# Finishing two blocks of a four-block quad as one pair, and a third seven-product quad in every chunk: attention folded into a squared-ReLU feed-forward layer

## The chip, the cores and the metric

The kernel runs on one core of one Trainium2 chip. The number that counts is the device time of one launch in microseconds (us). Nothing is shared between cores, and the profile is one execution on the same core. The engines are TensorE (PE, with its weight loads shown as PEld), VectorE (DVE), ScalarE (ACT), GpSimd (POOL) and SyncE (SP, which issues most transfers). The granted clock of PE is listed in the profile as PEclk.

## The reference

For each of four batches with N = 6080 rows and C = 256 channels, an attention over channels is made, and its output goes through a feed-forward layer of width 2048:

```python
qn = q / (np.linalg.norm(q, axis=1, keepdims=True) + 1e-06)
kn = k / (np.linalg.norm(k, axis=1, keepdims=True) + 1e-06)
s = kn.transpose(0, 2, 1) @ qn / tau
a = np.exp(s - s.max(-1, keepdims=True))
a /= a.sum(-1, keepdims=True) + 1e-09
x = v @ a                      # 24320 x 256 in all
h = x @ w_in                   # 256 -> 2048
r = np.maximum(h, 0.0)
return (r * r) @ w_out         # 2048 -> 256
```

## The kernel before, in words

The attention matrix (256 x 256 per batch) is folded into `w_in`, so the long part is two matrix products over 24320 tokens, here called the first and the second layer. Every float32 operand is split into a high and a low part; one product of two tiles is three matmuls (high x high, low x high, high x low).

**Chunks and quads.** Tokens come in 24 chunks, six to a batch: five of 2 x 512 tokens and one of 2 x 480. A chunk has eight quads (index j = 0 to 7). A quad is a 2 x 2 grid of blocks of the hidden layer: two sets of 128 hidden units by two halves of the tokens, called 11, 12, 21, 22. The first layer makes the four blocks with seven products instead of eight (Strassen's way, in Winograd's form): the functions `m1`, `m7`, `m6`, `m2`, `m5`, `m4`, `m3`, in this order, each of three matmuls (`product`, L384). They run in PSUM: `B` and `H` in the two `h` banks, `X` in the bank `x` and `Z` in the bank `z`. `X` and `Z` start as copies of `B`, made by ACT (L447 after `m1`, L455 after `m6`), then further products add to them. `X` ends as block 11 (after `m2`), `Z` as block 12 (after `m3`). Blocks 21 and 22 are made by DVE from a bank and the saved product `m7` (L472).

**Finishing a block.** `block` (L387 to 398) takes 11 or 12 by itself: Relu out of PSUM (L394, ACT), Square (L395, ACT), the high part (L396, ACT), the low part (L397, DVE). Blocks 21 and 22 are one pair of 2 x 512 in `blocks` (L414 to 419): max-and-multiply on DVE (L417; on ACT for j = 6 and 7), high part on ACT, low part on DVE.

**Second layer.** A plain quad gives eight pieces of three matmuls each (`layer2`, L550 in `accumulate`): four blocks times two halves of the output, added up over the quads in four PSUM banks `o00`, `o01`, `o10`, `o11`. For some quads, those of `SJ = (0, 2, 4)` cut to the chunk's `KS`, Strassen's seven products are used for the second layer too: three in the quad's place (`layer2s`: M3, M2, M4), and four (M1, M5, M6, M7) that are added up over the chunk's such quads in an `h` bank and run later in the chunk (`run_later`). Their operands are kept in `D` tiles (`combos`) and split later (`split_later`, L436 and L437). I call such a quad an S quad and the others P quads. Before the change `KS` is 0 for chunks 0 and 1, 2 for chunks 2 to 17 (quads 0 and 2 are S) and 3 for the last batch, chunks 18 to 23 (quads 0, 2 and 4 are S).

**What sets the order.** `plan` is written out by hand: a quad's seven products with the previous quad's pieces at fixed places between them. Side work (scores and folding of the next batch, loads, splits) has due times in quads (`at`) and is put in by `run_side`. Then a list scheduler of the framework moves an instruction whose operands are not ready behind others of its engine; each engine runs its own list strictly in order and waits on semaphores. Buffers come from rotating pools; taking a buffer waits for its last reader.

Of the kernel before, what the change touches and what calls it, by code (L numbers as in the profile page):

```python
# [6 lines left out]
F32 = mybir.dt.float32  # L7
# [11 lines left out]
def tile_channel_attention_relu2_ffn(ctx, tc, kq, vT, tau, w_in, w_out, outT):  # L19
# [18 lines left out]
    DB = 3  # L38
    OB = 6
# [10 lines left out]
    ps_z = ctx.enter_context(tc.tile_pool(name="ps_z", bufs=1, space=bass.MemoryType.PSUM))  # L50
# [52 lines left out]
    def decode_w_in(g):  # L103
        tag = "sq" if g else "g1"
        W = work.tile([P, NH, 2, GW], F32, name=tag, tag=tag, bufs=2 if g else 3)
# [31 lines left out]
    def score_load(b, g, tag="kq"):  # L137
        t = work.tile([P, G, C2], F32, name=tag, tag=tag, bufs={"kq": KB, "g2": 2, "D": DB}[tag])
# [238 lines left out]
    KS = [0 if ci < 2 else 3 if ci >= (B - 1) * NCH else 2 for ci in range(len(chunks))]  # L377
# [9 lines left out]
    def block(q, c, ps, eng, hl=None):  # L387

        T = chunks[q[0]][2]
        r = work.tile([P, HMAX], F32, name="r")  # L390
        if hl is None:
            hl = work.tile([P, 2, HMAX], F32R, name="g1", bufs=3)
        with tc.high_priority():
            nc.scalar.activation(out=r[:, :T], in_=ps[:, :T], func=AF.Relu)  # L394
        nc.scalar.activation(out=r[:, :T], in_=r[:, :T], func=AF.Square)  # L395
        eng(out=hl[:, 0, :T], in_=r[:, :T])  # L396
        nc.vector.tensor_sub(out=hl[:, 1, :T], in0=r[:, :T], in1=hl[:, 0, :T])  # L397
        gs[q, c] = hl[:, 0], hl[:, 1]
        return r

    def strassen(q):
        ci, j = q
        return j in SJ[:KS[ci]]

    def blocks(q):
# [5 lines left out]
        hl = work.tile([P, 2, 2, HMAX], F32R, name="g2", tag="g2", bufs=2)  # L411
        h, l = hl[:, 0, :, :T], hl[:, 1, :, :T]
        if q[1] >= NJ - 2 and KS[q[0]]:
            nc.scalar.activation(out=s, in_=s, func=AF.Relu)  # L414
            nc.scalar.activation(out=s, in_=s, func=AF.Square)
        else:
            nc.vector.scalar_tensor_tensor(out=s, in0=s, scalar=0.0, op0=ALU.max, in1=s, op1=ALU.mult)  # L417
        nc.scalar.copy(out=h, in_=s)  # L418
        nc.vector.tensor_sub(out=l, in0=s, in1=h)  # L419
        for i, c in enumerate(("21", "22")):  # L420
            gs[q, c] = hl[:, 0, i], hl[:, 1, i]
# [3 lines left out]
    def combos(q):  # L425
# [7 lines left out]
        nc.vector.tensor_sub(out=t2, in0=state[q]["r11"][:, :T], in1=t1)  # L433

    def split_of(x, T, hl):
        nc.scalar.copy(out=hl[:, 0, :T], in_=x)  # L436
        nc.vector.tensor_sub(out=hl[:, 1, :T], in0=x, in1=hl[:, 0, :T])  # L437
        return hl[:, 0], hl[:, 1]

    def m1(q):  # L440
# [4 lines left out]
        st["X"] = ps_x.tile([P, HMAX], F32, name="x")  # L445
# [3 lines left out]
    def m6(q):  # L449
# [3 lines left out]
        st["Z"] = ps_z.tile([P, HMAX], F32, name="z")  # L453
# [25 lines left out]
    def m5(q):  # L479
# [358 lines left out]
```

## Time and profile before

| | us |
|---|---|
| median of three timed runs | 2158.8 (2157.32 to 2159.95) |
| profiled execution, device time | 2156.35 |
| its span (first to last instruction) | 2154.6 |
| PE busy in the span | 2139.2 |
| DVE busy | 1733.2 |
| ACT busy | 1659.3 |

The profiled execution lies 2.45 us under the median of the timed runs, and 1.75 us of it lie outside the span. A row of a group reads: line, engine, operation, tile written <- tiles read, shape, count, then the busy time and the mean of one in ns, then the idle time of the engine just before and who ended it. Matmuls overlap, so the mean of one matmul (389 ns) is its way through the array; the pace is the distance between starts. In the chain of waits a row is the start in us, how long the chain stayed there, and how many matmuls it passed.

### The profile page before, as it was taken

What the parts mean: (1) busy time and instruction counts of PE and PEld (TensorE: products, weight loads), DVE (VectorE), ACT (ScalarE), POOL (GpSimd) and SP (SyncE); (2) the same over time, 40 slices, a digit from 0 to 9 for tenths busy, and PEclk for the clock granted to TensorE, in tenths of its full rate; (3) what the DMA queues carried; (4) which work ended last, traced back from release to release, by engine and by line L of the source; (5) the groups of instructions that cost most, each with busy time, mean ns of one, the idle gap of its engine ahead of it and who ended that gap; (6) DMA issues with size and microseconds to landing.
All of it is one profiled execution on the core that took longest, in us unless ns stands there. A gap on an engine that the chain in (4) does not pass through costs nothing.

```text
span 2154.6 us, 27464 instructions
## 1 busy us (share of the span) xinstructions
PE 2139.2 (99%) x9758; PEld 1770.2 (82%) x9758; DVE 1733.2 (80%) x2492; ACT 1659.3 (77%) x2784; POOL 37.7 (2%) x69
## 2 busy tenths in 40 slices
PE   9999999999999999999999999999999999999999
PEld 8778888888888888888888888888888888888887
DVE  6898888787787988878779798897877877878876
ACT  6677778787787877877778878787777778778776
POOL 0111000000000000000000000000000000000000
PEclk9999999999999999999999999999999999999999
DMA  9768655355765655546667555554655654555542
GB/s 357 278 229 316 234 199 201 137 206 209 261 241 180 220 196 199 178 155 230 211 217 258 201 199 211 183 188 153 215 213 203 231 199 170 195 189 180 188 171 87
DMA packets 123176, 446.26 MB, mean 207 GB/s; under 512 B 12928, under 2 KB 29824, under 8 KB 123040
## 3 DMA queue, kind: packets, MB, share of 16 engines
q1 hardware_dynamic: 115744, 406.11, 53.3%
q0 software_dynamic: 7296, 38.41, 4.7%
q8 instruction: 77, 1.26, 0.2%
q14 instruction: 59, 0.48, 0.1%
HBM read 381.16 MB, written 63.31 MB: 206 GB/s over the span
## 4 chain that ended last, share of the span: by engine, by line
PE 94%; ACT 3%; DVE 2%; DMA 0%; issue 0%; SPq 0%; ACTq 0%; DVEq 0%
PE o L550 39%; PE h L384 23%; PE z L384 12%; PE h L550 6%; PE x L384 6%; PE h L173 4%; PE h L292 2%; PE x L173 2%; ACT g L418 0%; DVE s L472 0%; ACT r L394 0%; DMA kq<-kq 0%; DVE hl L85 0%; ACT r L395 0%; ACT g L396 0%
## 5 line engine op out<-in xcount | busy, mean ns | idle before, releaser
L550 PE MATMUL o<-g,wo 128*128 128x512 f32 (+1 forms) x3858 | 1003.9, 389 | 3.7 <-ACT g L418 2.4
L550 PEld LDWEIGHTS o<-g,wo 128*128 128x128 f32 x3858 | 719.3, 188 | 162.4 <-DVE g L419 10.8
L384 PE MATMUL h<-vt,wt 128*128 128x512 f32 (+1 forms) x2304 | 625.2, 389 | 1.2 <-ACT x L447 0.4
L384 PEld LDWEIGHTS h<-vt,wt 128*128 128x128 f32 x2304 | 430.8, 188 | 95.3 <-ACT uM L580 4.2
L397 DVE TENSOR_TENSOR g<-r,g 128x512 fp32r<-128x512 f32 (+1 forms) x384 | 260.6, 681 | 117.1 <-ACT g L396 114.7
L384 PE MATMUL z<-vt,wt 128*128 128x512 f32 (+1 forms) x1152 | 326.3, 390 | 0.9 <-DVE s L472 0.5
L419 DVE TENSOR_TENSOR g<-s,g 128x1024 fp32r<-128x1024 f32 (+1 forms) x142 | 172.1, 1212 | 119.4 <-ACT g L418 119.3
L394 ACT ACTIVATE r<-z 128x512 f32<-128x512 f32 (+1 forms) x192 | 113.5, 591 | 188.1 <-PE z L384 187.5
L384 PEld LDWEIGHTS z<-vt,wt 128*128 128x128 f32 x1152 | 209.9, 188 | 43.8 <-DVE s L472 4.5
L395 ACT ACTIVATE r<-r 128x512 f32<-128x512 f32 (+1 forms) x384 | 240.4, 629 | 5.9
L396 ACT CAST g<-r 128x512 fp32r<-128x512 f32 (+1 forms) x368 | 225.6, 616 | 5.2
L418 ACT CAST g<-s 128x1024 fp32r<-128x1024 f32 (+1 forms) x142 | 147.4, 1038 | 39.3 <-DVE s L417 39.1
L384 PE MATMUL x<-vt,wt 128*128 128x512 f32 (+1 forms) x576 | 161.9, 388 | 0.0
L455 ACT COPY z<-h 128x512 f32<-128x512 f32 (+1 forms) x192 | 110.9, 578 | 36.8 <-PE h L384 35.7
L384 PEld LDWEIGHTS x<-vt,wt 128*128 128x128 f32 x576 | 108.1, 188 | 21.7
L394 ACT ACTIVATE r<-x 128x512 f32<-128x512 f32 (+1 forms) x192 | 113.9, 593 | 14.5 <-DVE D L433 9.3
L153 DVE TENSOR_TENSOR acc<-acc,sq 128x1024 f32<-128x1024 f32 x92 | 112.2, 1220 | 15.6 <-ACT sq L152 13.5
L371 DVE TENSOR_TENSOR vt<-v,vt 128x512 fp32r<-128x512 f32 (+1 forms) x144 | 95.4, 681 | 35.8 <-ACT vt L370 35.7
L417 DVE SCALAR_TENSOR_TENSOR s<-s 128x1024 f32<-128x1024 f32 (+1 forms) x98 | 118.3, 1207 | 0.2
L447 ACT COPY x<-h 128x512 f32<-128x512 f32 (+1 forms) x192 | 111.5, 580 | 3.7 <-PE h L384 3.1
L467 ACT COPY m<-h 128x512 f32<-128x512 f32 (+1 forms) x192 | 111.6, 581 | 1.7 <-PE h L384 0.6
L472 DVE TENSOR_TENSOR s<-z,m 128x512 f32<-128x512 f32 (+1 forms) x142 | 96.6, 680 | 14.7 <-PE z L384 11.6
(154 smaller groups left out, 2406.5 us busy)
## 6 DMA issues: line engine op xcount, KB each, us to landing
wt<-wsc SPq DMA_DIRECT2D x184, 896.0 KB, 4.7
wo<-wop SPq DMA_DIRECT2D x134, 512.0 KB, 5.3
kq<-kq SPq DMA_DIRECT2D x87, 512.0 KB, 5.2
wsc<-wt POOLq DMA_DIRECT2D x32, 896.0 KB, 5.5
v<-vT SPq DMA_DIRECT2D x40, 512.0 KB, 5.2
outT<-uM SPq DMA_DIRECT2D x80, 256.0 KB, 3.3
wo<-wos SPq DMA_DIRECT2D x50, 384.0 KB, 3.5
wo<-wodM SPq DMA_DIRECT2D x64, 256.0 KB, 4.4
```

The costliest lines, as they stand in the source:

```text
L153: nc.vector.tensor_add(out=accs[b], in0=accs[b], in1=sq)
L173: nc.tensor.matmul(out=s[:, h * C:(h + 1) * C], lhsT=l, rhs=r, start=first and h == 0 and n == 0, stop=last and n == len(terms) - 1, skip_ ...
L384: nc.tensor.matmul(out=out[:, :T], lhsT=w[:, l, i], rhs=v[:, r, :T], start=start and n == 0, stop=n == 2, skip_group_check=True)
L394: nc.scalar.activation(out=r[:, :T], in_=ps[:, :T], func=AF.Relu)
L395: nc.scalar.activation(out=r[:, :T], in_=r[:, :T], func=AF.Square)
L396: eng(out=hl[:, 0, :T], in_=r[:, :T])
L397: nc.vector.tensor_sub(out=hl[:, 1, :T], in0=r[:, :T], in1=hl[:, 0, :T])
L417: nc.vector.scalar_tensor_tensor(out=s, in0=s, scalar=0.0, op0=ALU.max, in1=s, op1=ALU.mult)
L418: nc.scalar.copy(out=h, in_=s)
L419: nc.vector.tensor_sub(out=l, in0=s, in1=h)
L467: nc.scalar.copy(out=state[q]["m7"][:, :T], in_=H[:, :T])
L550: nc.tensor.matmul(out=o[:, :T], lhsT=l, rhs=r[:, :T], start=start and k == 0, stop=stop and k == 2)
```

## The change

Four things change together.

1. `X` and `Z` become the two halves of one two-bank tile `x`. Block 11 is no longer finished after `m2`. After `m3`, the last product, one Relu of 2 x 512 takes both out of PSUM, one Square follows, and `pair` makes high and low parts for both (L396, L397, L403, L404 of the changed kernel). The next quad's first copy into `X` now waits for that Relu. The buffers for it: `g2` has three instead of two, `s` two instead of one, a new `t4` takes the extra operand of an S quad, and `g1` and `r` are gone.
2. The products of a quad stand in the order m1, m7, m6, m5, m4, m2, m3.
3. The pieces of the second layer are a queue (`waiting`): after a P quad four pieces stay behind for the quad after the next, after an S quad two. The part that is run is spread over three places, three eighths after `m7`, a quarter after `m6`, the rest after `m4`. `load_wo` is issued 0.4 quads later, the four later products of a chunk are due at 5.7, 6.4, 7.1 and 7.8 quads.
4. `KS` is 3 for every chunk from the third on, so chunks 2 to 17 have three S quads instead of two. The third operand of a later product goes into a `kq` buffer.

The core of the diff:

```diff
-    ps_z = ctx.enter_context(tc.tile_pool(name="ps_z", bufs=1, space=bass.MemoryType.PSUM))
...
-    KS = [0 if ci < 2 else 3 if ci >= (B - 1) * NCH else 2 for ci in range(len(chunks))]
+    KS = [0 if ci < 2 else 3 for ci in range(len(chunks))]
...
+    def squares(x, out, eng):
+
+        if eng is nc.vector:
+            nc.vector.scalar_tensor_tensor(out=out, in0=x, scalar=0.0, op0=ALU.max, in1=x, op1=ALU.mult)
+        else:
+            nc.scalar.activation(out=out, in_=x, func=AF.Relu)
+            nc.scalar.activation(out=out, in_=out, func=AF.Square)
+
+    def pair(q, x, cs):
+        T = chunks[q[0]][2]
+        hl = work.tile([P, 2, 2, HMAX], F32R, name="g2", tag="g2", bufs=GB)
+        h, l = hl[:, 0, :, :T], hl[:, 1, :, :T]
+        nc.scalar.copy(out=h, in_=x)
+        nc.vector.tensor_sub(out=l, in0=x, in1=h)
+        for i, c in enumerate(cs):
+            gs[q, c] = hl[:, 0, i], hl[:, 1, i]
...
     def m1(q):
...
-        st["X"] = ps_x.tile([P, HMAX], F32, name="x")
+        st["XZ"] = ps_x.tile([P, 2, HMAX], F32, name="x")
+        st["X"], st["Z"] = (st["XZ"][:, i] for i in range(2))
...
     def m2(q):
         product(q, A12, state[q]["X"], False)
-        state[q]["r11"] = block(q, "11", state[q]["X"], nc.scalar.copy if KS[q[0]] else nc.vector.tensor_copy)
...
     def m3(q):
         product(q, S4, state[q]["Z"], False)
         T = chunks[q[0]][2]
+        r = work.tile([P, 2, HMAX], F32, name="s", tag="s", bufs=2)
+        with tc.high_priority():
+            squares(state[q]["XZ"][:, :, :T], r[:, :, :T], nc.scalar)
+        pair(q, r[:, :, :T], ("11", "12"))
         if strassen(q):
...
+            t2, t1 = kept[q][:, 0, :T], kept[q][:, 1, :T]
+            nc.vector.tensor_sub(out=t2, in0=r[:, 0, :T], in1=t1)
+            nc.vector.tensor_sub(out=r[:, 1, :T], in0=r[:, 1, :T], in1=t2)
+            hl = work.tile([P, 2, HMAX], F32R, name="t4", tag="t4", bufs=1)
+            gs[q, "t4"] = split_of(r[:, 1, :T], T, hl[:, 0], hl[:, 1])
...
-        for m, t in zip(MS, {0: (), 2: (3.9, 4.7, 5 + MID, 6.2), 3: (5 + MID, 6.2, 6.8, 7 + MID)}[KS[ci]]):
+        for m, t in zip(MS, {0: (), 3: (5.7, 6.4, 7.1, 7.8)}[KS[ci]]):
...
-            at(n - 0.2, load_wo, ci, j)
+            at(n + 0.2, load_wo, ci, j)
...
-    plan = (m1, m7, ("11", 0), ("11", 1), m6, m2, ("21", 0), ("21", 1), m5, m4, ("22", 0), ("22", 1), ("12", 0),
-            m3, ("12", 1))
...
+    plan = (m1, m7, 0, m6, 1, m5, m4, 2, m2, m3)
+    waiting = []
     for n in range(len(quads) + 1):
         q = quads[n] if n < len(quads) else None
         p = quads[n - 1] if n else None
...
+        if p:
+            waiting += ([(layer2s, p, m) for m in ("M3", "M2", "M4")] if strassen(p) else
+                        [(layer2, p, c, e) for c in ("21", "22", "11", "12") for e in range(NH)])
+        todo = max(0, len(waiting) - (2 if p and strassen(p) else 4)) if q else len(waiting)
+        parts = [todo * 3 // 8, todo // 4]
+        parts.append(todo - sum(parts))
```

How it stands on the engines, at the step from quad 2 (S) to quad 3 (P) of chunk 20, in the last batch, where the number of products is the same before and after. PE before: `z_16847` is quad 2's block 12 (its last product `m3`), `h_16898` is `B` of quad 3, `x_16902` and `z_16919` its `X` and `Z`.

```order
L384 MATMUL z_16847<-vt_16616,wt_16719 128x512 x3
L384 MATMUL h_16898<-vt_16320,wt_16793 128x512 x3
L384 MATMUL h_16904<-vt_16362,wt_16793 128x512 x3
L550 MATMUL o10_16803<-g1_16813,wo_16734 128x512 x3
L550 MATMUL o00_16765<-g1_16853,wo_16807 128x512 x3
L384 MATMUL h_16898<-vt_16415,wt_16793 128x512 x3
L384 MATMUL x_16902<-vt_16580,wt_16793 128x512 x3
L550 MATMUL o11_16818<-g1_16813,wo_16734 128x512 x3
L384 MATMUL z_16919<-vt_16589,wt_16793 128x512 x3
```

PE now: the first row is quad 2's `m3` into the second half of its `x` tile; `h_15993` is `B` of quad 3, `x_15997` its two-bank tile, first used by `m5` in its `Z` half.

```order
L384 MATMUL x_15925<-vt_15726,wt_15818 128x512 x3
L384 MATMUL h_15993<-vt_15453,wt_15893 128x512 x3
L384 MATMUL h_15999<-vt_15486,wt_15893 128x512 x3
L545 MATMUL o00_15905<-g2_15918,wo_15873 128x512 x3
L384 MATMUL h_15993<-vt_15531,wt_15893 128x512 x3
L545 MATMUL o01_15966<-g2_15918,wo_15873 128x512 x3
L545 MATMUL o10_15936<-g2_15918,wo_15873 128x512
L384 MATMUL x_15997<-vt_15692,wt_15893 128x512 x3
L384 MATMUL h_15993<-vt_15720,wt_15893 128x512 x3
```

Between `m6` and `m5` there stood six matmuls (`m2` and a piece); now four matmuls of pieces stand there, and between `m3` and the next `m6` there are nine instead of twelve. ACT at the same place before (`r_16890` is block 12 of quad 2, `r_16924` block 11 of quad 3):

```order
L394 ACTIVATE r_16890<-z_16847 128x512
L395 ACTIVATE r_16890<-r_16890 128x512
L447 COPY x_16902<-h_16898 128x512
L467 COPY m7_16908<-h_16904 128x512
L396 CAST g2_16889<-r_16890 128x512
L455 COPY z_16919<-h_16898 128x512
L394 ACTIVATE r_16924<-x_16902 128x512
```

and now (`s_15982` holds blocks 11 and 12 of quad 2):

```order
L396 ACTIVATE s_15982<-x_15925 128x1024
L441 COPY x_15997<-h_15993 128x512
L459 COPY m7_16003<-h_15999 128x512
L397 ACTIVATE s_15982<-s_15982 128x1024
L448 COPY x_15997<-h_15993 128x512
L403 CAST g2_15985<-s_15982 128x1024
```

The copy into `X` (L441) stands directly behind a Relu of twice the width, and the Square of twice the width now stands ahead of the copy into `Z` (L448), which `m5` needs. Counted over the whole program, the matmuls of 512 columns go from 7269 to 7230 and those of 480 from 1413 to 1404.

More of the change, by code (lines that the diff above doesn't have):

```diff
@@ L38, in tile_channel_attention_relu2_ffn @@
     DB = 3
+    GB = 3
     OB = 6
@@ L103, in decode_w_in @@
     def decode_w_in(g):
-        tag = "sq" if g else "g1"
-        W = work.tile([P, NH, 2, GW], F32, name=tag, tag=tag, bufs=2 if g else 3)
+        tag = "sq" if g else "t4"
+        W = work.tile([P, NH, 2, GW], F32, name=tag, tag=tag, bufs=2 if g else 1)
         decode_f64(raws.pop(("in", g)), W.rearrange("p h t f -> p (h t) f"))
@@ L137, in score_load @@
     def score_load(b, g, tag="kq"):
-        t = work.tile([P, G, C2], F32, name=tag, tag=tag, bufs={"kq": KB, "g2": 2, "D": DB}[tag])
+        t = work.tile([P, G, C2], F32, name=tag, tag=tag, bufs={"kq": KB, "g2": GB, "D": DB}[tag])
         n = G if b or g else 1
@@ L282, in fold @@
         if ch == 0:
-            tag, n = ("kq", KB) if b or g else ("s", 1)
+            tag, n = ("kq", KB) if b or g else ("s", 2)
             us[b, g] = work.tile([P, NH, 2, GW], F32, name=tag, tag=tag, bufs=n)
@@ L385, in product @@
                              stop=n == 2, skip_group_check=True)
[L387 to L399, printed above, removed]
     def strassen(q):
@@ L410, in blocks @@
         s = state[q]["s"][:, :, :T]
[L411 to L421, printed above, removed]
+        squares(s, s, nc.scalar if q[1] >= NJ - 2 and KS[q[0]] else nc.vector)
+        pair(q, s, ("21", "22"))
     kept = {}
@@ L428, in combos, with split_of @@
         D = kept[q]
-        t2, t1, g22 = (D[:, i, :T] for i in range(3))
+        t1, g22 = D[:, 1, :T], D[:, 2, :T]
         s = D[:, 1:3, :T]
-        nc.vector.scalar_tensor_tensor(out=s, in0=s, scalar=0.0, op0=ALU.max, in1=s, op1=ALU.mult)
+        squares(s, s, nc.vector)
         nc.vector.tensor_sub(out=t1, in0=t1, in1=g22)
[L433 to L438, printed above, removed]
+    def split_of(x, T, h, l):
+        nc.scalar.copy(out=h[:, :T], in_=x)
+        nc.vector.tensor_sub(out=l[:, :T], in0=x, in1=h[:, :T])
+        return h, l
     def m1(q):
@@ L484, in m5 @@
         else:
-            state[q]["s"] = work.tile([P, 2, HMAX], F32, name="s", tag="s", bufs=1)
+            state[q]["s"] = work.tile([P, 2, HMAX], F32, name="s", tag="s", bufs=2)
         plus_m7(q, 1, state[q]["Z"])
@@ L559, in split_later @@
             hl = work.tile([P, 2, 2, HMAX], F32R, name="hl", tag="hl", bufs=HB)
-            hls = [hl[:, k] for k in range(K)]
+            hls = [hl[:, k] for k in range(2)]
+            hls += [work.tile([P, 2, HMAX], F32R, name="kq", tag="kq", bufs=KB) for _ in range(K - 2)]
         later[ci, m] = []
@@ L566, in split_later @@
                 nc.vector.tensor_sub(out=x, in0=x, in1=D[:, 2, :T])
-            later[ci, m].append(split_of(x, T, hl))
+            later[ci, m].append(split_of(x, T, hl[:, 0], hl[:, 1]))
     def run_later(ci, m):
@@ L604, in layer2 @@
         f, n = int(c[0]) - 1, int(c[1]) - 1
-        last = j == NJ - 1 and c in ("21", "12")
+        last = j == NJ - 1 and c[0] == "1"
         o, first = bank(n, e)
@@ L669, in tile_channel_attention_relu2_ffn @@
         attnT(0)
-        fold(0, 0, 0, ps_z.tile([P, HMAX], F32, name="z"))
+        fold(0, 0, 0, s0z)
         fold(0, 0, 1)
@@ L796, in tile_channel_attention_relu2_ffn @@
         p = quads[n - 1] if n else None
-        for k, step in enumerate(plan):
-            t = n + k / len(plan)
+        if p:
[4 more added lines that the diff above has]
+        parts.append(todo - sum(parts))
+        steps = []
+        for step in plan:
             if callable(step):
                 if q:
-                    mark(t, step, q)
-            elif p and strassen(p):
-                fn, *args = FOLLOWS.get(step, (None,))
-                if fn:
-                    mark(t, fn, p if fn is layer2s else quads[n - 2], *args)
-            elif p and not (q and strassen(q) and step[0] == "12"):
-                mark(t, layer2, p, *step)
+                    steps.append((step, q))
+            else:
+                steps += waiting[:parts[step]]
+                del waiting[:parts[step]]
+        for k, (fn, *args) in enumerate(steps):
+            t = n + k / len(steps)
+            mark(t, fn, *args)
             run_side(t)
```

12 lines of the change are left out of this document (1 added, 11 removed).

## The prediction

> **What bounds the kernel now.** I read the page first: the busy times, the granted clock, and by which engine the chain that ended last runs.
>
> ```profile
> span 2154.6 us, 27464 instructions
> PE 2139.2 (99%) x9758; PEld 1770.2 (82%) x9758; DVE 1733.2 (80%) x2492; ACT 1659.3 (77%) x2784; POOL 37.7 (2%) x69
> PEclk9999999999999999999999999999999999999999
> PE 94%; ACT 3%; DVE 2%; DMA 0%; issue 0%; SPq 0%; ACTq 0%; DVEq 0%
> ```
>
> PE sets the time, at a clock of nine tenths or more in every slice, and the chain is 94% PE. A busy share hides short waits, because a matmul's busy time overlaps its neighbours'. So the second view is the chain of waits in order of time, for the pace from start to start and for the length of a chunk and of a batch:
>
> ```profile
> 637.36 1.43 PE h L173 x12
> ...
> 1168.62 1.43 PE h L173 x12
> ...
> 1645.46 1.30 PE h L384 x6
> 1646.76 1.30 PE o L550 x6
> ...
> 1770.48 0.68 PE z L384 x3
> 1771.16 0.68 PE h L384 x3
> 1771.84 1.36 PE o L550 x6
> ...
> 1786.21 1.64 PE o L550 x6
> ...
> 1866.22 1.62 PE o L550 x6
> ```
>
> A matmul of 512 columns takes 1.36 / 6 = 0.2267 us, one of 480 columns 1.30 / 6 = 0.2167, one of the scores 1.43 / 12 = 0.119. A chunk of the last batch is 1866.22 - 1786.21 = 80.01 us. It holds 168 first-layer matmuls, 120 of five P quads, 27 of three S quads and 36 of the later products, 351 in all: 351 x 0.2267 = 79.57, so PE idles 0.44 us in it, and 0.28 of this is the one row of 1.64 where six matmuls should take 1.36. A batch before that is 1168.62 - 637.36 = 531.26 us. Its chunks hold 354 (two S quads: 168 + 144 + 18 + 24): five times 354 x 0.2267, 354 x 0.2167, 48 folding matmuls x 0.2267 and 288 of the scores x 0.119 make 523.2. So 8.1 us are idle in six chunks, 1.35 each. Chunks 2 to 23 together: 16 x 1.35 + 6 x 0.44 = 24, of which I count 20, since folds and norms keep some of their own waits. The third view, the waits, says on whom:
>
> ```profile
> PEld o L550 <- DVE g L419: 10.8, 36, 0.4
> PEld o L550 <- ACT g L418: 6.3, 13, 1.6
> PEld z L384 <- DVE s L472: 4.5, 15, 0.9
> PEld h L384 <- ACT uM L580: 4.2, 10, 0.5
> PE o L550 <- ACT g L418: 2.4, 3, 1.1
> ```
>
> (us in total, times, longest.) The three rows of L418 and L419, 19.5 us in the whole program, are pieces of the second layer that arrive before the parts of blocks 21 and 22 are ready. None of the others is half as large as the first.
>
> **Step 1, products saved.** Sixteen chunks get a third S quad. It replaces eight pieces by three and adds one product to each of four later ones: eight to seven, three matmuls less a chunk. The counts of the order say 39 fewer of 512 columns and 9 fewer of 480: 39 x 0.2267 + 9 x 0.2167 = **-10.8 us**, since PE sets the time. Only waits can take that away.
>
> **Step 2, pieces that run later.** After a P quad four pieces stay behind, twelve matmuls or 2.7 us more for the parts of 21 and 22. The longest wait of the rows above is 1.6, so those waits go where the queue really is four deep; after an S quad it is two, and the waits on L472 and L580 are untouched. Of 20 us of idle time, none to all may go. I take half, **-10 us**, because the L418 and L419 rows are the larger part of what is listed, but the whole program's first two chunks own a share of them.
>
> **Step 3, the hand-over.** Now `X` and `Z` leave PSUM only after `m3`, by one Relu of twice the width, and the next quad's copy into `X` waits for it; ahead of the copy into `Z` stands the wide Square. I price this with rows of the timeline:
>
> ```profile
> 1200.08 0.84 PE L384 MATMUL z<-vt,wt 128*128 128x512 f32 x3
> 1200.96 0.60 ACT L394 ACTIVATE r<-z 128x512 f32<-128x512 f32 x1 [2.05 <-PE z L384]
> 1202.40 0.58 ACT L447 COPY x<-h 128x512 f32<-128x512 f32 x1
> 1202.91 0.62 ACT L395 ACTIVATE r<-r 128x512 f32<-128x512 f32 x1
> ...
> 1213.11 1.06 ACT L415 ACTIVATE s<-s 128x1024 f32<-128x1024 f32 x1
> 1214.07 0.58 ACT L394 ACTIVATE r<-z 128x512 f32<-128x512 f32 x1
> ...
> 77.76 0.60 ACT L455 COPY z<-h 128x512 f32<-128x512 f32 x1
> 78.41 0.96 PE L384 MATMUL z<-vt,wt 128*128 128x512 f32 x3 [0.29 <-ACT z L455]
> ```
>
> ACT starts 1200.96 - 1200.08 = 0.88 us after the first of three matmuls, or 0.43 after the last. A next ACT instruction of 512 starts 0.51 after the one before; behind one of 1024 it starts 0.96 later. PE starts 78.41 - 78.36 = 0.05 after the copy ends. No Relu of 1024 out of PSUM is in this trace: twice the busy 0.60 would be 1.20, the 1024-wide row from SBUF is 1.06, and 0.60 plus 512 columns at the difference of 0.60 to 1.06 is 1.06 less a little; I take 1.02 to 1.06, bounds 1.0 to 1.2. Clock zero is `m3`'s first matmul of an S quad, in the order shown above. Relu 0.88 to 1.90, copy `X` 1.93 to 2.51, copy `m7` from 2.44, Square 2.92 to 3.97, copy `Z` 3.87 to 4.45, and PE can start `m5` at 4.50. On PE: `m6` is the twelfth matmul after `m3`'s first, due at 2.72, 0.16 after its copy: no wait. `m5` stands 19 matmuls on, due at 19 x 0.2267 = 4.31: a wait of 0.19. With the bounds of the Relu (and the Square alike) it is 0.15 to 0.5. This happens at 0 to 1, 2 to 3 and 4 to 5: 0.57 a chunk. After a P quad eight pieces are to be run, five of them ahead of `m5` instead of a handful of matmuls, and there is no wait.
>
> From a P quad to an S quad (1 to 2, 3 to 4) the slow side is DVE, in the order the bank additions, the subtraction for `t4`, the max-and-multiply of the pair and `t4`'s low part, which frees the `s` buffer that the next Relu writes:
>
> ```profile
> 1198.38 0.68 DVE L472 TENSOR_TENSOR s<-h,m 128x512 f32<-128x512 f32 x1
> 1198.97 0.68 DVE L437 TENSOR_TENSOR hl<-D,hl 128x512 fp32r<-128x512 f32 x1
> 1199.57 1.22 DVE L417 SCALAR_TENSOR_TENSOR s<-s 128x1024 f32<-128x1024 f32 x1
> 1200.71 0.68 DVE L437 TENSOR_TENSOR hl<-D,hl 128x512 fp32r<-128x512 f32 x1
> ```
>
> 0.59 for a 512, 1.14 for a 1024. Counted on from the wide high part of the S quad, which ACT ends at 5.45, its low part holds DVE to 6.65, two of 512 to 7.83, the max to 9.0, and ACT's high part ends at 10.1. The first piece that reads it is the 45th matmul, due at 10.2 + 0.19. The slack is 0.3, less than one more 512 on DVE (0.59), and DVE gets further work here from the later products and the tokens of the next chunk. I price the two steps at 0.2 each, between 0 and 0.6: with 0.57 about 1.0 us a chunk. In chunks 2 to 17 four bursts of score matmuls (288 in 24 bursts of 1.43 us a batch) fall in eight quads and cover the wait where they fall ahead of it: 0.6. Sum: 6 x 1.0 + 16 x 0.6 = **+15.6 us**, with the ends of both, 0 and 40.
>
> **Step 4, the rest.** ACT: six instructions of 512 per quad become three of 1024; DVE gains the splits of 64 more later operands.
>
> ```profile
> L395 ACT ACTIVATE r<-r 128x512 f32<-128x512 f32 (+1 forms) x384 | 240.4, 629 | 5.9
> L419 DVE TENSOR_TENSOR g<-s,g 128x1024 fp32r<-128x1024 f32 (+1 forms) x142 | 172.1, 1212 | 119.4 <-ACT g L418 119.3
> L418 ACT CAST g<-s 128x1024 fp32r<-128x1024 f32 (+1 forms) x142 | 147.4, 1038 | 39.3 <-DVE s L417 39.1
> L397 DVE TENSOR_TENSOR g<-r,g 128x512 fp32r<-128x512 f32 (+1 forms) x384 | 260.6, 681 | 117.1 <-ACT g L396 114.7
> ```
>
> ACT saves 192 x (6 x 0.61 - 3 x 1.04) = 104 and gains about 40 in splits and in the high parts of chunks 0 and 1: some 64 less, 74%. DVE saves 192 x (2 x 0.681 - 1.212) = 29; a third S quad in 16 chunks costs it nine more instructions of 512 (four splits, five sums) less one low part of 1024, 16 x (9 x 0.681 - 1.212) = 79, and some 7 go to ACT with chunks 0 and 1: 43 more, 82%. Both lie beside PE; without that cover 43 us would show. Loads move by 0.4 of a quad, some 4 us of the 10 that a quad takes; the piece that needs the weights runs a quad later too, so I cost it at 0. The start and chunks 0 and 1: 0, within 4 either way.
>
> The Trainium skill speaks against step 3 ("Perfetto Trace Analysis", "Optimizing Scalar/DVE Operations"): larger operations help an engine that is saturated, while engines that are not saturated but cause bubbles elsewhere do better with instructions broken up. ACT at 77% is not saturated, and the trace agrees so far that 0.96 after a wide instruction stands against 0.51. By that rule the first rival below is right.
>
> **Sum.** -10.8 - 10 + 15.6 = -5.2 us against the profiled 2156.35, so about 2151 there; the timed runs lie 2.45 above the profiled one: 2158.8 - 5.2 = **2153.6 us**.
>
> **Rivals.**
> - *Slower: the in-order ACT.* Each hand-over waits for a Relu, a Square and a high part of about 1 us each, in one line with the three copies that PE needs; one late instruction ahead of them passes on its whole delay. Five hand-overs with an S quad in 22 chunks make 110. The gains of steps 1 and 2 are 20.8, so 20.8 / 110 = 0.19 us each is the point from which it is slower. At 0.30 each, which the Relu's upper bound gives: 33 - 20.8 = +12, 2171 us. For it: the 0.19 wait that I found by hand, with no stray instruction. Against it: ACT has a quarter of its time free.
> - *The whole gain.* The framework's scheduler puts side work and later products at these places, and 0.19 is less than one matmul; then nothing of step 3 remains but a third: -10.8 - 10 + 4 = -17, 2142 us. For it: later products are 36 matmuls a chunk. Against: the order at 2 to 3 shows none of them there.
> - *DVE eats it.* Its 82% is a mean. Chunks 2 to 17 have scores, splits and a third S quad; if a tenth of the 43 us has no cover there, 4 us of the 5.2 are given back: 2158 us, no change. For it: 16 of the 22 chunks are of this kind. Against: 18% are free, and the pieces that wait four behind even it out.
> - That the matmuls aren't removed is excluded by the counts.
>
> **How the numbers follow.** A measurement here tells 0.2%, 4.3 us, from no change. My forecast has 0.45 with its own range 2149 to 2160, the slower rival 0.24, the whole gain 0.20, DVE 0.11. Faster: 0.26 of the 0.45, and 0.20: 0.46. The same: 0.19 and 0.11: 0.30. Slower: 0.24. The range reaches from near the whole gain to just short of the slower rival at 0.30 each, 2142 to 2170; by the far bound of step 3 it would be 2178, outside.
>
> **What would show it.** Step 1: 48 fewer matmuls at the same 0.2267. Step 2: the rows for pieces waiting on high and low parts of the 21 and 22 pair fall below 10 us. Step 3: new rows for `m5` (L384 into `x`) waiting on the copy L448, and for pieces waiting on the wide high part, 12 to 20 us together, and a last-batch chunk of 80.0 to 80.6 us. If that chunk is 79.7, the whole gain is right; if over 81, the slower rival. If DVE is busy over 95% in chunks 2 to 17, the third is. The forecast is wrong if chunks 2 to 17 gain less than the last batch, which saves no matmul, or if the three rows of step 2 stay.

## The result, and the profile after

The changed kernel takes **2182.3 us** (2179.7 to 2182.9) against 2159.0: a ratio of 1.0106, 95% interval 1.0089 to 1.0124. It is 23 us slower. The forecast was 2153.6 with a range of 2142 to 2170, so the forecast had the sign wrong, and the time lies outside its range. The profiled executions differ by 2181.1 - 2154.6 = 26.5 us of span, since the one of before lies under its median. The page of the changed kernel, span, engines and the chain by engine:

```profile
span 2181.1 us, 26984 instructions
PE 2155.1 (99%) x9710; PEld 1755.7 (80%) x9710; DVE 1766.1 (81%) x2412; ACT 1618.8 (74%) x2288; POOL 37.4 (2%) x69
PE 90%; ACT 5%; DVE 3%; DMA 1%; issue 1%; SPq 0%; ACTq 0%; DVEq 0%
```

The 48 matmuls are gone (9758 to 9710), ACT does 40 us less work, and yet ACT's share of the chain rises from 3 to 5% and PE's falls from 94 to 90%. The waits (us in total, times, longest) say where:

```profile
ACT s L396 <- PE x L384: 207.4, 72, 6.2
PEld x L384 <- ACT x L448: 37.5, 113, 1.4
PEld h L384 <- ACT x L441: 18.1, 44, 2.2
PEld o L545 <- ACT g L403: 8.4, 16, 1.7
ACT hl L277 <- DMA kq<-wins: 6.8, 3, 2.3
PE h L384 <- ACT x L441: 6.7, 5, 1.8
PEld o L545 <- DVE g L404: 3.8, 14, 0.3
PE o L545 <- ACT g L403: 2.2, 4, 1.2
```

The three rows for pieces that wait on their pair fell from 19.5 (L418, L419) to 14.4 (L403, L404, now for all four blocks), but two new ones stand at the top: `m5` behind the copy into `Z` (L448), 113 times, and `m6` behind the copy into `X` (L441). And one row was nowhere before: ACT waits for a transfer of folding weights (L277).

The chunks put this in order. I took the start of every chunk's first product from the trace (times in us; "the three" are chunks 5, 11 and 17, the last of a batch, in whose course the next batch's weights are folded; "the others" are the other thirteen of chunks 2 to 17). The kernels other than the first two are the experiments below; the median of before moves between 2158.1 and 2160.2 from one of their sessions to the next.

| kernel | chunk 2 starts | the three | the others | 18 to 22 | median |
|---|---|---|---|---|---|
| before | 252.3 | 249.8 | 1165.3 | 400.4 | 2159 |
| changed | 255.0 | 263.6 | 1164.5 | 408.4 | 2182.3 |
| e1, two S quads | 254.8 | 253.8 | 1170.2 | 408.5 | 2178.5 |
| e2, two in chunks 4, 10, 16 | 253.7 | 253.1 | 1166.2 | 408.5 | 2173.4 |
| e3, third S quad alone | 253.9 | 246.8 | 1152.2 | 399.8 | 2141.2 |
| e4, single Relus | 253.5 | 255.8 | 1163.9 | 406.0 | 2169.3 |
| e5, single Relu and Square | 246.7 | 249.3 | 1168.1 | 405.9 | 2164.0 |
| e6, piece more before `m5` | 255.1 | 255.2 | 1160.8 | 413.3 | 2176.9 |
| e7, later products earlier | 255.4 | 253.4 | 1163.5 | 409.0 | 2172.6 |
| e8, short queue | 259.6 | 260.5 | 1200.5 | 428.2 | 2241.7 |
| e9, e5, e7 and `m2` early | 250.8 | 250.9 | 1160.4 | 404.1 | 2157.1 |
| e10, e3 with later products later | 254.0 | 246.9 | 1157.6 | 400.8 | 2147.9 |
| e11, e3 again | 252.8 | 246.8 | 1152.2 | 399.9 | 2140.7 |
| e12, later products moved, before | 253.8 | 248.6 | 1164.6 | 399.8 | 2152.3 |

Between before and the changed kernel: the start and chunks 0 and 1 take 2.7 us more although twelve matmuls (four pieces, 2.7 us) are not yet done there, so 5.4 us are lost; the three chunks lose 13.8, and 2.0 of saved matmuls on top, 15.8; the others gain 0.8 where 8.8 were saved, 8.0 lost; chunks 18 to 22, which save nothing, lose 8.0. With the 10.8 saved: 5.4 + 15.8 + 8.0 + 8.0 - 10.8 = 26.4 of the 26.5 us. The first of these is the least sure: before, e3, e10, e11 and e12 run the same chunks 0 and 1, and their chunk 2 starts anywhere from 252.3 to 254.0. The other columns agree within 0.1 us where a kernel was run twice (e3 and e11).

**The hand-over.** The last batch shows it undisturbed. The step from quad 2 to quad 3 in chunk 20, timeline of the changed kernel:

```profile
1873.49 1.32 PE L384 MATMUL x<-vt,wt 128*128 128x512 f32 x5
1874.85 1.03 ACT L396 ACTIVATE s<-x 128x1024 f32<-128x1024 f32 x1 [3.62 <-PE x L384]
1875.91 0.57 ACT L441 COPY x<-h 128x512 f32<-128x512 f32 x1
1876.39 0.59 ACT L459 COPY m<-h 128x512 f32<-128x512 f32 x1
1876.68 0.84 PE L384 MATMUL h<-vt,wt 128*128 128x512 f32 x3
1876.87 1.07 ACT L397 ACTIVATE s<-s 128x1024 f32<-128x1024 f32 x1
1877.83 0.60 ACT L448 COPY x<-h 128x512 f32<-128x512 f32 x1
1878.48 0.97 PE L384 MATMUL x<-vt,wt 128*128 128x512 f32 x3
```

`m3` begins at 1873.95 (the third of the five matmuls of the first row). Relu at +0.90, copy `X` +1.96, copy `m7` +2.44, Square +2.92, copy `Z` +3.88, `m5` +4.53: within 0.03 of the forecast's 0.88, 1.93, 2.44, 2.92, 3.87 and 4.50. `m5` was due at 4.31, so it waits 0.22. What I had left out is the row's end: three matmuls of a product that waited take 0.97 in the timeline, those of `m6` 0.84. The start of the second one is 0.34 behind the first instead of 0.23, so a wait costs 0.11 more than its length. By the starts of the matmuls this step costs 0.21 + 0.11 = 0.32, and the three such steps of chunks 18 to 22 cost 0.31 each in the mean. The other term of the forecast is seen in the step from quad 1 to quad 2, where a piece waits for the wide high part of 21 and 22 (L403):

```profile
1866.84 1.22 PEld L545 LDWEIGHTS o<-g,wo 128*128 128x128 f32 x6 [0.51 <-ACT g L403]
```

PE loses 0.55 in quad 2 of such a chunk and 0.10 in quad 4, where 0.2 was forecast for each. The chunk's length, from the chain of waits:

```profile
1764.91 1.36 PE h L384 x6
...
1846.67 1.36 PE h L384 x6
...
1928.41 1.36 PE h L384 x6
```

81.76 and 81.74 us against 80.01, so 1.7 us a chunk (1.6 by the table, over five) where I expected 80.0 to 80.6; I had written that over 81 the slower rival is right.

**The late load.** Chunk 5's first quad, timeline of the changed kernel (SPq is the transfer's issue):

```profile
517.45 1.29 SPq L271 DMA_DIRECT2D kq<-wins  x1
...
524.00 1.05 ACT L277 CAST hl<-kq 128x1024 fp32r<-128x1024 f32 x1 [2.25 <-DMA kq<-wins]
...
525.45 1.04 ACT L403 CAST g<-s 128x1024 fp32r<-128x1024 f32 x1
...
526.88 1.01 ACT L396 ACTIVATE s<-x 128x1024 f32<-128x1024 f32 x1
...
528.09 0.56 ACT L441 COPY x<-h 128x480 f32<-128x480 f32 x1
...
528.71 1.99 PE L384 MATMUL h<-vt,wt 128*128 128x480 f32 x6 [1.70 <-ACT x L441]
```

The same load in the kernel before:

```profile
485.31 0.77 SPq L271 DMA_DIRECT2D kq<-wins  x1
```

The load needs a `kq` buffer, and those are now also held by the third operand of the later products; it is issued 32 us later. (That the operand is the reason is what e1, e2 and e7 ask.) ACT stands for 2.25 us in front of the cast that needs it, and behind that cast queue the high part, the Relu and the copy for which PE then waits 1.7 us.

### The profile page after: what moved, and what is told of

It is laid out like the page before. It is cut to its first block, busy times and chain, and to the rows that moved or that the text cites. A ratio compares the mean times of both kernels' runs of the same rounds, so it can differ in the third digit from the quotient of the medians.

```text
span 2181.1 us, 26984 instructions
## 1 busy us (share of the span) xinstructions
PE 2155.1 (99%) x9710; PEld 1755.7 (80%) x9710; DVE 1766.1 (81%) x2412; ACT 1618.8 (74%) x2288; POOL 37.4 (2%) x69
## 4 chain that ended last, share of the span: by engine, by line
PE 90%; ACT 5%; DVE 3%; DMA 1%; issue 1%; SPq 0%; ACTq 0%; DVEq 0%
PE o L545 34%; PE h L384 21%; PE x L384 18%; PE h L545 8%; PE h L173 4%; PE h L292 2%; PE x L173 2%; ACT s L396 1%; ACT g L403 1%; ACT s L397 1%; DVE s L464 1%; ACT x L448 1%; DVE g L404 1%; ACT x L441 1%; DVE s L394 1%
## 5 line engine op out<-in xcount | busy, mean ns | idle before, releaser
L545 PE MATMUL o<-g,wo 128*128 128x512 f32 (+1 forms) x3420 | 890.1, 390 | 2.6 <-ACT g L403 2.2
L384 PE MATMUL x<-vt,wt 128*128 128x512 f32 (+1 forms) x1728 | 469.7, 396 | 5.7 <-ACT x L448 3.9
L404 DVE TENSOR_TENSOR g<-s,g 128x1024 fp32r<-128x1024 f32 (+1 forms) x318 | 383.4, 1209 | 93.5 <-ACT g L403 88.5
L384 PEld LDWEIGHTS x<-vt,wt 128*128 128x128 f32 x1728 | 311.7, 188 | 95.0 <-ACT x L448 37.5
L403 ACT CAST g<-s 128x1024 fp32r<-128x1024 f32 (+1 forms) x318 | 330.3, 1043 | 48.8 <-DVE s L394 47.1
L396 ACT ACTIVATE s<-x 128x1024 f32<-128x1024 f32 (+1 forms) x192 | 195.1, 1016 | 219.6 <-PE x L384 207.4
L397 ACT ACTIVATE s<-s 128x1024 f32<-128x1024 f32 (+1 forms) x236 | 249.4, 1057 | 1.1
L448 ACT COPY x<-h 128x512 f32<-128x512 f32 (+1 forms) x192 | 112.5, 586 | 2.5 <-PE h L384 0.6
L441 ACT COPY x<-h 128x512 f32<-128x512 f32 (+1 forms) x192 | 111.7, 582 | 2.1
L545 PE MATMUL h<-kq,wo 128*128 128x512 f32 (+1 forms) x408 | 109.8, 389 | 0.0
L173 PE MATMUL h<-hl 128*128 128x256 f32 x720 | 103.2, 282 | 0.0
```

The lines of the kernel that those rows point to most:

```text
L173: nc.tensor.matmul(out=s[:, h * C:(h + 1) * C], lhsT=l, rhs=r, start=first and h == 0 and n == 0, stop=last and n == len(terms) - 1, skip_ ...
L384: nc.tensor.matmul(out=out[:, :T], lhsT=w[:, l, i], rhs=v[:, r, :T], start=start and n == 0, stop=n == 2, skip_group_check=True)
L396: nc.scalar.activation(out=out, in_=x, func=AF.Relu)
L397: nc.scalar.activation(out=out, in_=out, func=AF.Square)
L403: nc.scalar.copy(out=h, in_=x)
L404: nc.vector.tensor_sub(out=l, in0=x, in1=h)
```

## The experiments

**e1: two S quads in chunks 2 to 17** in the changed kernel. Their later products keep the due times of the change (a second line of the edit, in e2 too).

```diff
-    KS = [0 if ci < 2 else 3 for ci in range(len(chunks))]
+    KS = [0 if ci < 2 else 3 if ci >= (B - 1) * NCH else 2 for ci in range(len(chunks))]
```

> The changed kernel with two S quads instead of three in chunks 2 to 17, as before the change; everything else of the change stays. In the trace of the changed kernel PE's idle time between matmuls is 75 us against 39 before: 28 against 20 in the start and chunks 0 and 1, 17 against 2 in chunks 5, 11 and 17, 10 against 3 in the last batch, 20 against 13 in the other thirteen chunks. Theory 1 (a load of weights for folding that waits for a kq buffer, held by the third operand of a later product, costs 15 us; the rest is the hand-over): without the third operand the 15 us go, 10.8 us of matmuls come back, some 3 us of hand-overs go: 2182 - 15 + 10.8 - 3 = 2175 us. Theory 2 (only the hand-over from quad to quad costs): 78 hand-overs next to an S quad instead of 110, 29 us x 32 / 110 = 8 us less and 10.8 more: 2185 us.

Measured: 2178.5 us, 1.0085 (1.0070 to 1.0100) of before, between the two and nearer the first. By the table the three chunks give back 9.8 us, though their matmuls come back too, and the others lose 5.7 where 8.8 come back. So the late load hangs on the third operand, and parts 1 to 3 of the change alone cost 18 us. (The 8 us that the text above gives to the start are 5.4 by the starts of the chunks, with the spread named there.)

**e2: two S quads in chunks 4, 10 and 16 only,** the chunks before the three.

```diff
-    KS = [0 if ci < 2 else 3 for ci in range(len(chunks))]
+    KS = [0 if ci < 2 else 2 if ci % NCH == 4 and ci < (B - 1) * NCH else 3 for ci in range(len(chunks))]
```

> The changed kernel with two S quads in chunks 4, 10 and 16 alone, whose later products run while the weights for folding are loaded; three elsewhere. Theory 1 (late load): the wait of 1.9 us at the start of chunks 5, 11 and 17 and what follows it go, about 12 of the 15 us, and 3 x 0.68 = 2 us of matmuls come back: 2182 - 12 + 2 = 2172 us. Theory 2 (hand-over alone): 2182 + 2 - 2 = 2182 us, no difference.

2173.4 us, 1.0062 (1.0045 to 1.0079): theory 1. The three chunks fall from 263.6 to 253.1 though nothing in them was changed; the load is issued at 488.7 and the row of ACT waiting for it is gone.

**e3: the third S quad alone,** on the kernel before.

```diff
-    KS = [0 if ci < 2 else 3 if ci >= (B - 1) * NCH else 2 for ci in range(len(chunks))]
+    KS = [0 if ci < 2 else 3 for ci in range(len(chunks))]
...
-            hls = [hl[:, k] for k in range(K)]
+            hls = [hl[:, k] for k in range(2)]
+            hls += [work.tile([P, 2, HMAX], F32R, name="kq", tag="kq", bufs=KB) for _ in range(K - 2)]
```

> The kernel before with three S quads in chunks 2 to 17, and the third operand of a later product in a kq buffer, as in the change; blocks 11 and 12 finished singly, the old order and the old places of the pieces. Theory 1 (late load): 2159 - 10.8 + 10 to 15 for the load, about 2160 us, no gain. Theory 2 (hand-over alone): the gain of the products is kept, 2159 - 10.8 + 2 = 2150 us.

2141.2 us, 0.9911 (0.9897 to 0.9926), the fastest of all: 19 us under before and 41 under the changed kernel. Both theories missed. Its page:

```profile
span 2139.5 us, 27507 instructions
PE 2124.1 (99%) x9710; PEld 1764.7 (82%) x9710; DVE 1799.4 (84%) x2620; ACT 1692.6 (79%) x2848; POOL 37.7 (2%) x69
PE 96%; DVE 2%; ACT 1%; DMA 0%; issue 0%; SPq 0%; ACTq 0%; DVEq 0%
```

The chain is 96% PE, with ACT and DVE busier than in the kernel before and in the changed one (1692.6 and 1799.4): more work on them did not keep this kernel from being the fastest. The folding load comes at 496.6 us, late, but in time. So the operand in `kq` harms only together with something else of the change, and a part of the gain is not matmuls; e7 and e12 ask for the two.

**e4: single Relus.** `X` and `Z` get tiles of their own again; one Relu of 512 after `m2` (the first added line), one after `m3`.

```diff
+            nc.scalar.activation(out=r[:, 0, :T], in_=state[q]["X"][:, :T], func=AF.Relu)
...
-            squares(state[q]["XZ"][:, :, :T], r[:, :, :T], nc.scalar)
+            nc.scalar.activation(out=r[:, 1, :T], in_=state[q]["Z"][:, :T], func=AF.Relu)
+            nc.scalar.activation(out=r[:, :, :T], in_=r[:, :, :T], func=AF.Square)
```

> The changed kernel with X and Z in tiles of their own again: a Relu of 512 on X after m2 and one on Z after m3; the wide Square, the wide high and low parts, the queue of pieces and the three S quads stay. Theory of step 3 (the wide Relu stands ahead of the copies that PE needs): at the step from an S quad to a P quad the Relu ends at 1.48 instead of 1.90 after the first matmul of m3, and the copy into Z some 0.4 earlier; the 13 us that m5 waits in quads 1, 3 and 5 fall to about 3 and the start gives back some 4 us: 2182 - 14 = 2168 us. Rival (it is the wide Square ahead of the copy into Z, not the Relu): under 4 us, 2178 to 2182 us.

2169.3 us, 1.0041 (1.0026 to 1.0056): the expected number, but not for the expected reason. Timeline, quad 2 to quad 3 of chunk 20:

```profile
1863.28 0.60 ACT L490 ACTIVATE s<-z 128x512 f32<-128x512 f32 x1
1863.91 1.06 ACT L491 ACTIVATE s<-s 128x1024 f32<-128x1024 f32 x1
...
1864.87 0.58 ACT L441 COPY x<-h 128x512 f32<-128x512 f32 x1
...
1865.51 0.97 PE L385 MATMUL h<-vt,wt 128*128 128x512 f32 x3
```

The Square moved ahead of the copy into `X`, and it is now `m6` that waits (0.97 again). In 18 to 22 only 2.4 us came back; 7.8 came from the three chunks. The load of folding weights is nearly as late there as in the changed kernel (issued at 515.1) and ACT waits 6.7 us for it in all, against 6.8 there; that it costs PE less because a shorter queue stands behind it on ACT is a guess. The rival had the kind of mechanism, a wide instruction ahead of a copy, though not the size.

**e5: single Relu and single Square,** the one on `X` in `m2`, the one on `Z` in `m3`; the high and low parts are still wide. The edit is shown against e4. The two Squares also stand outside the `high_priority` block in which the change had put the Square, so e5 undoes its width and its priority together.

```diff
+        nc.scalar.activation(out=r[:, 0, :T], in_=r[:, 0, :T], func=AF.Square)
...
-            nc.scalar.activation(out=r[:, :, :T], in_=r[:, :, :T], func=AF.Square)
+        nc.scalar.activation(out=r[:, 1, :T], in_=r[:, 1, :T], func=AF.Square)
```

> As the run with single Relus, and the Square of 512 on X ahead of m3 and on Z behind the copies; the high and low parts of blocks 11 and 12 stay wide. With single Relus the hand-over kept its cost: m5 waited less, but m6 waited 10 us in quads 1 and 3, since the wide Square stood ahead of the copy into X. Theory (any instruction of 1 us ahead of the copies): now Relu 0.88 to 1.48, copy X 1.56 to 2.14, m7 to 2.8, Square to 3.4, high part to 4.3, copy Z to 4.83, m5 due at 4.99: the 15 us of waits in quads 1, 3 and 5 fall to about 2, 2169 - 13 = 2156 us. Rival (the hand-over is set by DVE or by the weights, not by ACT's order): 2166 to 2169 us.

2164.0 us, 1.0023 (1.0014 to 1.0033): 5 less than e4, of 13 expected. The profiled executions lie 8.9 apart, since that of e5 is the fastest of its ten: the start and chunks 0 and 1 give back 6.8, the three chunks 6.5, and the others lose 4.2. The same hand-over, timeline:

```profile
1856.86 1.05 ACT L404 CAST g<-s 128x1024 fp32r<-128x1024 f32 x1
1857.81 0.58 ACT L449 COPY z<-h 128x512 f32<-128x512 f32 x1
...
1858.44 0.96 PE L385 MATMUL z<-vt,wt 128*128 128x512 f32 x3
```

The wide high part is the next wide instruction ahead of the copy into `Z`, and `m5` waits as before. `m3` was at 1853.35, so the copy came at +4.46 and ended at +5.04, where I had +4.83.

**e6: one piece more between `m6` and `m5`,** wherever five, six or seven pieces are due. That is quads 1, 3 and 5, which the text below has in mind, and quads 2, 4 and 6 as well, where six are due.

```diff
-        parts = [todo * 3 // 8, todo // 4]
+        parts = [todo * 3 // 8, (todo + 3) // 4]
```

> The changed kernel with one piece more between m6 and m5 where the queue has five to seven pieces, that is after an S quad (1, 2, 2 instead of 1, 1, 3). Theory (m5 comes too early for the copy into Z): copy Z ends at 5.33 in the order that results, m5 is due 24 matmuls after m3, 5.44: the 13 us of m5 in quads 1, 3 and 5 go and nothing else changes, 2182 - 13 = 2169 us. Rival (ACT's chain is longer than PE's quad, so a wait only moves to the next place): 2179 to 2183 us.

2176.9 us, 1.0082 (1.0067 to 1.0097), between the two. Waits of e6:

```profile
PEld x L384 <- ACT x L448: 20.8, 56, 1.4
PEld h L384 <- ACT x L441: 19.8, 72, 1.6
PEld o L545 <- ACT g L403: 14.0, 21, 1.6
PEld o L545 <- DVE g L404: 5.5, 23, 0.3
```

`m5` waits half as often, but `m6` (L441) 72 times instead of 44, and the pieces on their high part 14.0 us instead of 8.4. By quads (chunks 2 to 23, from the starts of the matmuls), PE's idle time in quads 1 and 3 fell from 11.8 to 3.6 us and that in quad 4 rose from 5.2 to 19.5. Chunks 18 to 22 are 5 us longer than in the changed kernel; what e6 gains comes from the three chunks (8.4 us), where the load is issued at 504.5, and from the other thirteen (3.7). A wait taken away in one place comes back at another, as the rival has it, though at another price. But the edit isn't as small on PE as the text above has it: the list scheduler made a new order of it. In quad 4 of chunks 18 to 22 only three matmuls of pieces stand ahead of `m5`, where the changed kernel has fifteen, so this run can't tell what the old order with one piece moved would do.

**e7: the later products due earlier,** at the 5.46, 6.2, 6.8 and 7.46 quads that the kernel before had for chunks with three S quads.

```diff
-        for m, t in zip(MS, {0: (), 3: (5.7, 6.4, 7.1, 7.8)}[KS[ci]]):
+        for m, t in zip(MS, {0: (), 3: (5 + MID, 6.2, 6.8, 7 + MID)}[KS[ci]]):
```

> The changed kernel with the later products of a chunk due as before the change (5.46, 6.2, 6.8, 7.46 quads instead of 5.7, 6.4, 7.1, 7.8). The load of folding weights is issued at 517 us in the changed kernel, at 497 with the third S quad alone and at 485 before. Theory (the kq buffer is held longer because the later products come later): the load comes in time, 2182 - 10 = 2172 us, like the run with two S quads in chunks 4, 10 and 16. Rival (the buffer is held by something else): 2180 to 2183 us.

2172.6 us, 1.0063 (1.0048 to 1.0078): the theory. The load's row, and ACT in the same quad, without a wait for it:

```profile
503.31 0.54 SPq L271 DMA_DIRECT2D kq<-wins  x1
```

```profile
524.80 1.02 ACT L396 ACTIVATE s<-x 128x1024 f32<-128x1024 f32 x1
525.71 0.55 ACT L459 COPY m<-h 128x480 f32<-128x480 f32 x1
526.16 0.57 ACT L441 COPY x<-h 128x480 f32<-128x480 f32 x1
```

The three chunks lose 10.2 us of their excess and nothing else moves by more than 1. So it takes both, the operand in `kq` and the later due times, and something of the rest of the change too: e10 has both in the kernel before, and there the load is issued at 498.7 and in time. What the third condition is was not tried.

**e8: a short queue,** one piece behind after a P quad, none after an S quad.

```diff
-        todo = max(0, len(waiting) - (2 if p and strassen(p) else 4)) if q else len(waiting)
+        todo = max(0, len(waiting) - (0 if p and strassen(p) else 1)) if q else len(waiting)
```

> The changed kernel with a short queue: one piece stays behind after a P quad and none after an S quad, instead of four and two. It prices step 2, pieces that run later. If the queue hides the waits on the pairs as the prediction had it, about 10 us or more are lost: 2192 us or above. Rival (the old places of the pieces would do as well): 2180 to 2186 us.

2241.7 us, 1.0384 (1.0368 to 1.0399), 59 us over the changed kernel. Waits of e8:

```profile
PEld x L384 <- ACT x L448: 43.8, 93, 1.7
PEld o L545 <- ACT g L403: 41.6, 89, 1.3
PEld o L545 <- DVE g L404: 18.9, 69, 1.5
PEld h L384 <- ACT m L459: 15.0, 18, 1.3
```

Without the queue the pieces arrive at pairs that aren't ready. By the starts of the matmuls 27 of the 59 us are lost ahead of pieces in chunks 2 to 23, the rest mostly ahead of `m6` and `m4`. This isn't the old order either: in e8's queue the pieces of 21 and 22 can stand directly behind `m7`, where the kernel before has two pieces, `m6` and `m2` first, and the changed one two pieces and `m6`. So it shows that the changed kernel needs its queue, not that the queue takes old waits away.

**e9: e5 and e7 together, and `m2` ahead of the pieces behind `m6`.**

```diff
-    plan = (m1, m7, 0, m6, 1, m5, m4, 2, m2, m3)
+    plan = (m1, m7, 0, m6, m2, 1, m5, m4, 2, m3)
```

> The changed kernel with three causes taken away together: Relu and Square of 512 and own tiles for X and Z (2164 us alone), the later products due as before (10 us less alone), and m2 ahead of the pieces behind m6, so that more matmuls stand ahead of m5. If the causes add up: 2164 - 10 for the load - up to 8 of the 16 us that m5 still waits in quads 1, 3 and 5 = 2146 to 2154 us, under the kernel before. If they don't (a wait that goes comes back at the next place): 2158 to 2164 us. In both cases it does not reach the third S quad alone, 2141 us, because the wide high part stays ahead of the copy into Z.

2157.1 us, 0.9996 (0.9986 to 1.0005): no difference from before, between the two cases. The hand-over in quads 1, 3 and 5 is nearly clean (`m5` waits about 2 us there in all, against 17 in e5), but quad 4 has 10 us; there too the order of PE is another, with seven matmuls of pieces ahead of `m5` instead of fifteen. Undoing the three causes gives back the 23 us that the change had cost. What e9 keeps (the wide high and low parts, the queue, the order of the products, the later `load_wo`) costs about the 16 us by which e3 is faster; which of these does was not tried.

**e10: e3 with the change's due times** (5.7, 6.4, 7.1, 7.8).

> The kernel before with the third S quad (2141 us) and the later products due as in the change, 5.7, 6.4, 7.1 and 7.8 quads. The third quad alone keeps 2 us of waits at the first later product, whose third operand is made in quad 4, and 4 us of pieces in quad 4. Theory (that operand comes too late): 2 to 4 us less, 2137 to 2139 us; the load of folding weights is issued some 10 us later than the 497 us of that run, still ahead of its use near 524. Rival (the load gets late as in the changed kernel): 2150 us.

2147.9 us, 0.9948 (0.9932 to 0.9965), 7 over e3: wrong in sign, and the rival's mechanism isn't there either, as the load stands at 498.7. In e10 PE waits at quad 2 of chunks 6 and 12 for first-layer weights:

```profile
614.37 0.80 SPq L331 DMA_DIRECT2D wt<-wsc  x2
...
620.58 1.65 PE L384 MATMUL h<-vt,wt 128*128 128x512 f32 x6 [1.42 <-DMA wt<-wsc]
```

Two loads of weights leave together, just ahead of the output transfers. That explains 3 of the 7 us; why the queue of SP stood until then was not tried, and the rest is spread over the chunks.

**e11: e3 once more.**

> The third S quad alone once more, beside the two others on the same chip: 2141 us.

2140.7 us, 0.9916 (0.9901 to 0.9931).

**e12: the kernel before with its later products moved.**

```diff
-    2: (3.9, 4.7, 5 + MID, 6.2)
+    2: (5 + MID, 6.2, 6.8, 7 + MID)
```

> The kernel before with its two S quads, and only the due times of the later products in chunks 2 to 17 moved from 3.9, 4.7, 5.46 and 6.2 quads to the 5.46, 6.2, 6.8 and 7.46 that the third S quad brings. The third S quad alone gained 18 to 19 us, 10.8 of them matmuls; in its trace PE idles 5 us less in chunks 2 to 23. Theory (the rest comes from the moved products, which no longer crowd quad 4): 2159 - 5 = 2154 us. Rival (it comes from quad 4 being an S quad itself): 2158 to 2160 us.

2152.3 us, 0.9969 (0.9957 to 0.9981), 6 under before, as the theory has it. By the medians it agrees with e3: 10.8 of matmuls and 6 from the due times make 17 of the 18 to 19 us. The trace shows less: its execution is the slowest of the six (2155.3), and in chunks 2 to 23 PE idles 16.5 us against 19.2 before and 13.3 in e3. So 3 to 6 us come from the due times; whether the rest comes from quad 4 being an S quad stays open.

## Why the prediction was wrong

- **Step 1, -10.8 us: right.** 48 fewer matmuls at the same pace; e3 keeps this gain, and some 6 us of PE's idle time go there as well, part of it by the due times that come with three S quads, which I had not seen.
- **Step 2, -10 us: failed.** PE's idle time ahead of pieces in chunks 2 to 23 was some 8 us before and is 7 to 9 after, by whether gaps under 0.02 us are counted. So 10 us were never there to take: the 19.5 us of the rows that I read are mostly waits of weight loads, not of PE. And the queue doesn't do what I wrote. `waiting` takes 21 and 22 first, so the four pieces that stay behind are always those of 11 and 12. Between `m4`, which completes 21 and 22, and their first piece there stand 27 matmuls before and 30 in the order of the queue now, three more and not twelve; in the trace of chunk 20 it is 26 from quad 3 to 4 and 20 from quad 1 to 2, where the list scheduler put them ahead of `M2` and PE waits for them. The room of the four pieces goes to the pair of 11 and 12, which is ready later, by `m3` and three wide instructions. So the cover that I counted against the old waits pays for the new lateness.
- **Step 3, +15.6 us: the mechanism right, the size short.** Each time in the chain of a hand-over from an S to a P quad came out within 0.03 us. Three things were missing. PE loses 0.11 us after a wait, so 0.31 a step was measured where I had 0.19; the row of 0.96 for three matmuls behind a wait, among my own rows, could have shown it. The two steps from a P to an S quad cost 0.65 a chunk where I had 0.4. And some 0.2 a chunk is lost in other places. Hand-over and queue together were to cost a net 5.6 us in chunks 2 to 23; without the late load they cost about 21 (8.0 in the last batch, 8.0 in the others and some 5 in the three). In the last batch, e4 to e6 gave back 2.4, 2.5 and -4.9 of the 8.0 us: the wait went from `m5` to `m6`, to the high part or to quad 4.
- **Step 4, loads at 0: failed.** I asked only whether the second-layer weights come in time. The third operand's buffer, and who else wants one, I did not follow. It cost 10 of the 15.8 us in chunks 5, 11 and 17 (e2 and e7). The shares of step 4 came out near: ACT has 40 us less work where I had 64, DVE 33 more where I had 43.
- **The start, 0 within 4: at the edge.** The two profiled executions give 5.4. But the five kernels with the old chunks 0 and 1 start chunk 2 at 253.4 in the mean and the changed kernel, e1, e2 and e7 at 254.7, which with the 2.7 of pieces not yet done makes 4. With a narrow Relu and Square and tiles of their own (e5) chunk 2 starts 8.3 us earlier, with the wide Square (e4) only 1.5. That it is the same in-order ACT, beside the decoding of the weights, fits this but wasn't shown: e9 has e5's narrow instructions and starts it 4.2 earlier.
- **The rivals.** The slower one, at 0.24, had the right engine and the right reason, and its price of 0.30 a hand-over is near the 0.31 measured from S to P and the 0.33 from P to S; it named 2171 us, and the late load is most of the rest. DVE as a bound is excluded by e3, which has more DVE work and is fastest; in chunks 2 to 17 of the changed kernel DVE is busy 84%. The whole gain failed for the reason of step 3.

The Trainium skill's rule ("Perfetto Trace Analysis", "Optimizing Scalar/DVE Operations": where an engine that is not saturated causes bubbles elsewhere, breaking its instructions up may let work be done sooner) is borne out for the whole kernel: ACT went from 77% to 74% busy and the kernel got slower, and breaking Relu and Square up again (e5) took 18 us off. In the last batch, away from the start and the late load, it gave back only 2.5 of the 8.0 us. I quoted it and gave the trace's agreement, and still left the slower case at 0.24.

What stays open: which of parts 1 to 3 costs what, as none was run alone on the kernel before, and with it the 16 us between e9 and e3; what quad 4 would do in e6 and e9 without the scheduler's new order; what besides the operand and the due times makes the load late; and the 4 us of e10 that the late weights don't explain.

## What to carry to other kernels

When PE sets the time, judge a fused instruction by what stands behind it in its engine's queue, not by the work that it saves: with 40 us less on ACT the kernel became 23 us slower. A slack that is spent to make one part of a change possible cannot be counted as a gain by another. And for every tile that a change puts into an existing pool, list the other users of the pool and the transfer that waits for the buffer: a load 32 us later showed only when a cast stood in front of the copies. When pieces are held back in a queue, look up which ones: here they were not the ones that had waited. Of a change with four parts, each part alone should be run: one part here is worth 19 us, and the other three, which were not run one by one, cost 41 on top of it.

## What the runs showed of the hardware

A product that had to wait takes 0.97 us for three matmuls in the timeline and one that had not 0.84: its second matmul starts 0.34 us behind the first, against a pace of 0.2267. The weight loads of the changed kernel at the same hand-over, for `m6`, which did not wait, and for `m5`:

```profile
1876.53 0.58 PEld L384 LDWEIGHTS h<-vt,wt 128*128 128x128 f32 x3
...
1878.48 0.53 PEld L384 LDWEIGHTS x<-vt,wt 128*128 128x128 f32 x3 [0.47 <-ACT x L448]
```

The load of `m6` begins at 1876.53, 0.15 ahead of its matmul at 1876.68, beside the matmul before it. The waiting product's load waits too and begins with its matmul at 1878.48. The loss behind a wait does not grow with the wait. In chunks 2 to 23, between matmuls of 512 columns, the second start was about 0.11 us late behind 32 of the 34 waits of 0.18 us or more in the changed kernel, and behind all 85 in e8, 14 of which lasted over 1 us; behind 172 of the 202 waits of 0.02 to 0.15 us in the changed kernel it was less than 0.08 us late. A Relu of 1024 columns out of two PSUM banks took 1.03 us, less than two of 0.60, as a sum by rows had it.
